# Columns by TensorE transpositions, Gram steps at other slots, idle products in the first inverse, and output copies in halves, in a delta-rule attention with an FFN

## The chip, the cores and the metric

The kernel runs on one core of one Trainium2 chip. The metric is the time of one execution on the device, in microseconds; three executions of the kernel before were timed, and one more was profiled. TensorE (PE) multiplies, VectorE (DVE) and ScalarE (ACT) do the elementwise work, GpSimd (POOL) next to nothing, and SyncE (SP) issues nearly all DMA transfers from one queue in order.

## The reference

Attention by the delta rule over 4 sequences of 768 tokens, 8 heads of 48 columns, and behind it a feed-forward layer (FFN) over all 3072 tokens, 384 to 2048 to 384:

```python
def _attn_ref(q, k, v, beta):
    k_n = k / (np.linalg.norm(k, axis=-1, keepdims=True) + 1e-06)
    state = np.zeros((B, H, D, D), dtype=np.float32)
    for t in range(S):
        kt, vt, bt = (k_n[:, :, t], v[:, :, t], beta[:, :, t, None])
        y[:, :, t] = np.einsum('bhd,bhde->bhe', q[:, :, t], state)
        v_old = np.einsum('bhde,bhd->bhe', state, kt)
        state = state + bt[:, :, :, None] * np.einsum('bhd,bhe->bhde', kt, vt - v_old)
    return y

def _moe_ref(x, w_in, w_out):        # x: the attention's y, heads side by side
    h = x @ w_in
    g = np.maximum(0.01 * h, h)
    return g @ w_out
```

## The kernel before

**Blocks.** The sequence is cut into 12 blocks of 64 tokens; a block takes these 64 tokens of all four sequences, so the FFN of a block n sees 256 tokens. For each block the steps are:

- *Gram* (`gram`, pg L284): products k k^T and k q^T of the block. ACT copies them (gs, L288), eight DMAs gd<-gs (L292) write the part for the inverse to DRAM, and two L<-gd (L307) read it back in the inverse's layout. For blocks 0 and 1 `first` does this.
- *Inverse* (`inv`): norms and scales (`norms`, L324 and on), a memset of the buffer T (L367; there is one T), then 31 elimination steps on VectorE (`eliminate`, L348 multiplies, L353 subtracts), each for the two 32 x 32 triangular halves of every head and sequence. At the end ACT copies T into the other layout (L402), and SP writes both to DRAM (td L409, tt L410). One inverse covers blocks 0 and 1 together, then there is one for each block.
- *Join* (`merge_z`, `merge_u`): SP reads tt and td back as block-diagonal tiles sq (four sq<-tt L466, four sq<-td L469) and into rt (L475); sixteen products pz and sixteen pu (`product`, L437) make the off-diagonal quarter of the inverse.
- *Solve* (`solve`): products pk, pw, pc, py (L561, L577, L587, L597) with copies on ACT between them (rt L563, rv L579 and L589), in two halves (g = 0 and 1) of the heads. The last gives y, which ACT copies into ys (L599), 128 tokens a half, 384 columns in fp32.
- *Columns* (`columns`): y has to stand with its columns on the partitions. Six fp32 products of 128 x 128, ys as the stationary operand and the unit matrix `eye` as the moving one, write px (L627; three column groups by two halves). ACT casts px to xh (L119), VectorE makes the rest xl = px - xh (L120), both fp32r.
- *FFN* (`ffn`): for each of 16 f, nine products ph of 256 columns (L656; xh and xl by the two parts of w_in), ACT makes gh (L661) and the leaky ReLU in place (L662), VectorE gl, the rest (L664); two f later six products po of 384 columns (L646), three for each half of the tokens, sum into po_0 and po_1. In the end ACT copies these into ob (L676), and four DMAs write the rows to the output (L679).

Weights come as 64-bit words and are cut into parts on VectorE and ACT (L144 to L177), some before the first FFN and the rest beside it.

**What sets the order.** `weave` calls the steps of several streams by slots: in the loop over n, 17 slots, one for each f and one for the end of the FFN. Beside the FFN of block n run the solve of block n + 1 (slots by SV), the inverse of block n + 2 (slots by IV, the entry n of it) and a Gram step for block n + 2 (slots by GG, for n = 0 to 2); from n = 2 on another Gram step, for block n + 3, runs at slot 12. `behind(name)` holds an instruction back until the last one so marked has been issued. From these calls a scheduler with a model of the engines makes the order in which every engine and queue runs; within an engine nothing overtakes.

The lines that set the slots are:

```python
IV, GG = ((7, 17), (8, 17), (8, 17), (2, 17)), ((0, 2), (3, 4), (1, 2))   # L731
SV = (0, 9), (3, 11), (2, 11)
```

Of the kernel before, what the change touches and what calls it, by code (L numbers as in the profile page):

```python
# [9 lines left out]
F32 = mybir.dt.float32  # L10
# [10 lines left out]
C = 64  # L21
# [9 lines left out]
HC = C // 2  # L31
P = 128
# [14 lines left out]
def delta_moe_kernel(ctx: ExitStack, tc, kq0, kqT, kv, qT, beta, cst, w_all, out, nblk):  # L47
# [10 lines left out]
    nc = tc.nc  # L58
    NFC, _, DO = w_all.shape[1:]
    NCC = DO // P  # L60
    NTB = TB // P
# [6 lines left out]
    ps_a = ctx.enter_context(tc.tile_pool(name="ps_a", bufs=4, space=PSUM))  # L68
# [6 lines left out]
    eye = csb[:, C:C + P]  # L75
# [5 lines left out]
    neg = st.tile([P, P], F32R, name="neg")  # L81
# [32 lines left out]
    def behind(name):  # L114

        return tc.issue_after(mark[name]) if name in mark else nullcontext()

    def split(src, hi, lo):
        mark["xh"] = nc.scalar.copy(hi, src).ins  # L119
        return nc.vector.tensor_tensor(lo, src, hi.bitcast(F32), ALU.subtract)  # L120
# [44 lines left out]
    def lows():  # L165
        while True:
            f, g, t = later.pop(0)
            if f in BYV:
                nc.vector.tensor_tensor(t[:, 2 * DO:], g, t[:, 0:2 * DO].bitcast(F32), ALU.subtract)
# [10 lines left out]
    Lh, gm, nrm, Tts, zs, ys, xs, done = {}, {}, {}, {}, {}, {}, {}, set()  # L180

    def need(gen, fn, n):
        while (fn, n) not in done:
            next(gen)
# [153 lines left out]
    def eliminate(b, L, j, T, m):  # L338


        w = HC - 1 - j
        parts = []
        for x in range(min(m, 2)):
            t = T[:, x:m:2]
            k = t.shape[1]
            tv = sb.tile([P, 144], F32, tag=f"tmp{x}", name=f"tmp{b}_{j}_{x}", bufs=1)
            tv = tv[:, 0:k * w].rearrange("p (x w) -> p x w", x=k)
            nc.vector.tensor_tensor(  # L348
                tv, t[:, :, j:j + 1].broadcast_to([P, k, w]),
                L[:, j, j + 1:].rearrange("p (o w) -> p o w", o=1).broadcast_to([P, k, w]), ALU.mult)  # L350
            parts.append((tv, t[:, :, j + 1:]))
        for tv, t in parts:
            mark["steps"] = nc.vector.tensor_tensor(t, t, tv, ALU.subtract).ins  # L353

    def inv(b):

        if b:
            need(gg, gram, NB[b][0])
        two = len(NB[b]) > 1
        M = HC if two else HC // 2  # L360
        X = sb.tile([P, HC * HC], F32, tag="T", name=f"T{b}", bufs=1)
        T = X[:, 0:M * HC].rearrange("p (m i) -> p m i", m=M)
        if two:
            nc.gpsimd.memset(T, 0.0)
        else:
            with behind("gl"):
                nc.vector.memset(T, 0.0)  # L367
        yield
        L = Lh.pop(b)
        c = norms(b, L.rearrange("p m i -> p (m i)")[:, ::HC + 1])  # L370
        if two:
            nc.vector.tensor_copy(X[:, ::HC + 1], c)
        else:
            for e in range(2):
                r = slice(e * 64, e * 64 + 64)
                nc.vector.tensor_copy(X[r, e:M * HC:HC + 2], c[r, e::2])
        for x in range(2):
            l = L[:, x * HC // 2:(x + 1) * HC // 2]
            nc.vector.tensor_tensor(l, l, c.rearrange("p (o i) -> p o i", o=1).broadcast_to(list(l.shape)), ALU.mult)
        if two:  # L380
            for n in NB[b]:
                lengths(n)
        yield
        for j in range(HC - 1):
            eliminate(b, L, j, T, j + 1 if two else j // 2 + 1)
            if j == HC - 2:
                if two:
                    Tc = sb.tile([P, HS, HC], F32, tag="L", name="tc", bufs=2)
                    nc.vector.transpose(Tc.rearrange("p l i -> p i l"), T.rearrange("p m i -> p i m"))
                    for i, n in enumerate(NB[b]):  # L390
                        Tts[n] = Tc, T[i * 64:i * 64 + HC]
                    for g in range(NGR):
                        place(0, g, 1)
                    d = nc.vector.transpose(T, T)
                    mark["inverse"] = d.ins
                    for g in range(NGR):
                        d = place(0, g, 0)
                    mark["inverse"] = d.ins
                else:
                    n = NB[b][0]  # L400
                    Tt = X[:, M * HC:].rearrange("p (i m) -> p i m", m=M)
                    nc.scalar.copy(Tt.rearrange("p i m -> p m i"), T)  # L402
                    td = dr.tile([2, HC, HS, HC], F32, tag="td", name=f"td{n}")
                    tt = dr.tile([HS, HC, HC], F32, tag="tt", name=f"tt{n}")
                    Tts[n] = td, tt
                    for x in range(2):
                        a = x * 64
                        for e in range(2):
                            nc.sync.dma_start(td[e, x::2].rearrange("m l i -> l m i"), T[a + e * HS:a + (e + 1) * HS])  # L409
                        nc.sync.dma_start(tt.rearrange("l i (x m) -> x l i m", m=M)[x], Tt[a:a + HS])  # L410
                done.add((inv, b))
            yield
# [119 lines left out]
    def solve(n):  # L532
        b = where[n][0]
        need(iv, inv, b)
        if n >= 2:
            lengths(n)
# [82 lines left out]
    def columns(n):  # L619

        need(sv, solve, n)
        xs[n] = parts = []
        px = [ps_a.tile([P, 2, TB], F32, tag="a", name=f"px{n}_{i}") for i in range(2)]
        part = [px[cc // 2][:, cc % 2] for cc in range(NCC)]
        for cc, x in enumerate(part):
            for g in range(NGR):
                i = nc.tensor.matmul(x[:, g * P:(g + 1) * P], ys[n, g][:, cc * P:(cc + 1) * P], eye, start=True, stop=True)  # L627
        mark["px"] = i.ins
        for cc, x in enumerate(part):
            xh, xl = (sb.tile([P, TB], F32R, tag=t, name=f"{t}{n}_{cc}", bufs=3) for t in ("xh", "xl"))  # L630
            i = split(x, xh, xl)
            if not n:
                mark["x"] = i.ins
            parts.append((xh, xl))

    def ffn(n):
        need(sv, solve, n)
        x = xs.pop(n)
        po = [ps_o.tile([P, 512], F32, tag=f"o{t}", name=f"po{n}_{t}") for t in range(NTB)]
        pend = []  # L640

        def second(f, gh, gl):
            for t in range(NTB):
                ts_ = slice(t * P, (t + 1) * P)
                for k, (a, w) in enumerate(((gh, wo[0]), (gh, wo[1]), (gl, wo[0]))):
                    i = nc.tensor.matmul(  # L646
                        po[t][:, :DO], a[:, ts_], w[f],
                        start=(f == 0 and k == 0), stop=(f == NFC - 1 and k == 2))
            mark["po"] = i.ins

        for f in range(NFC):
            ph = hbank[f % 2][:, f // 2 % 2]
            k = 0
            for cc in range(NCC):
                for a, e in ((wi[0], 0), (wi[0], 1), (wi[1], 0)):
                    i = nc.tensor.matmul(ph, a[f][:, cc * P:(cc + 1) * P], x[cc][e], start=(k == 0), stop=(k == 3 * NCC - 1))  # L656
                    k += 1
            mark["ph"] = i.ins
            gh = sb.tile([P, TB], F32R, tag="gh", name=f"gh{n}_{f}", bufs=FB)
            gl = sb.tile([P, TB], F32R, tag="gl", name=f"gl{n}_{f}", bufs=FB)  # L660
            nc.scalar.activation(gh, ph, AF.Prelu, alpha=0.01)  # L661
            i = nc.scalar.activation(ph, ph, AF.Prelu, alpha=0.01)  # L662
            mark["h"] = i.ins
            i = nc.vector.tensor_tensor(gl, ph, gh.bitcast(F32), ALU.subtract)  # L664
            mark["gl"] = mark[f"gl{f}"] = i.ins
            pend.append((f, gh, gl))
            if len(pend) > PD:
                second(*pend.pop(0))
            yield
        if n + 1 < nblk:  # L670
            columns(n + 1)
        for a in pend:
            second(*a)
        for t in range(NTB):
            ob = sb.tile([P, DO], F32, tag="ys", name=f"ob{n}_{t}", bufs=3)
            nc.scalar.copy(ob, po[t][:, :DO])  # L676
            for a in range(0, P, C):
                r0 = (t * P + a) // C * nblk * C + n * C
                nc.sync.dma_start(out[r0:r0 + C], ob[a:a + C])  # L679
        yield  # L680

# [45 lines left out]

WAHEAD, WEARLY = 4, 8
BYV = (0, 1) + tuple(range(3, 16, 2))
KA, KB, WB = 4, 2, 12  # L730
IV, GG = ((7, 17), (8, 17), (8, 17), (2, 17)), ((0, 2), (3, 4), (1, 2))  # L731
LL, AG = 2, 6
SV = (0, 9), (3, 11), (2, 11)
PD, FB = 2, 3
# [65 lines left out]
```

## Time and profile before

| | us |
|---|---|
| median of three runs (lowest, highest) | 657.07 (655.5, 658.13) |
| the profiled execution | 655.7 |
| its span from the first to the last instruction | 653.6 |
| TensorE busy | 602.4 (92%) |
| VectorE busy | 443.1 (68%) |
| ScalarE busy | 332.4 (51%) |

The mean granted clock of TensorE is 0.993 of full. The page cuts the span into 40 slices of 16.3 us; a digit is the busy share in tenths:

```
PE   5258999989979989999999999999999999999996
DVE  3999999987645969749749749659559559222221
```

TensorE is idle in part of the first 50 us, where the weights are cut, the first inverse runs and the first solve waits for it. From the fourth slice on it is near full, with thinner slices between 100 and 240 us, and it is full from 250 us to the end. VectorE is full in the first 145 us and then again in every inverse.

### The profile page before, as it was taken

To read this page: it belongs to the slowest core of one execution; us is meant where nothing else is said; L and a number is where in the kernel's file an instruction comes from. 1 tells how busy PE (TensorE), PEld (TensorE's weight loads), DVE (VectorE), ACT (ScalarE), POOL (GpSimd) and SP (SyncE) were. 2 spreads that over 40 slices of the span, in tenths; PEclk is the share of its full clock that TensorE was granted. 3 is DMA by queue.
4 is the path that set the end of the run, shared out by engine and by line. 5 is a ranking of instruction groups with operands and counts; after the bars stand their busy time and mean duration, and the time that the engine had idled before them with its cause. 6 is when DMAs were issued, how large, how long until landed. Compare 5 with 4: busy or idle time off the path is not lost.

```text
span 653.6 us, 19762 instructions
## 1 busy us (share of the span) xinstructions
PE 602.4 (92%) x7762; PEld 563.1 (86%) x7762; DVE 443.1 (68%) x1994; ACT 332.4 (51%) x855; POOL 10.7 (2%) x17
## 2 busy tenths in 40 slices
PE   5258999989979989999999999999999999999996
PEld 4156789988869979999999999999999999999996
DVE  3999999987645969749749749659559559222221
ACT  3456999334526445545545545445445445444322
POOL 6000000000000000000000000000000000000000
PEclk9998999999999999999999999999999999999999
DMA  5983953152453551461571660660660640400101
GB/s 122 292 252 115 242 203 75 26 121 35 100 99 56 132 96 30 87 128 41 107 122 28 118 134 3 119 134 4 126 127 7 123 78 15 75 19 2 26 0 25
DMA packets 124572, 59.51 MB, mean 91 GB/s; under 512 B 111424, under 2 KB 114624, under 8 KB 124480
## 3 DMA queue, kind: packets, MB, share of 16 engines
q1 hardware_dynamic: 124064, 57.73, 40.7%
q8 instruction: 61, 1.00, 0.7%
q10 hardware_dynamic: 416, 0.53, 0.4%
q14 instruction: 31, 0.25, 0.1%
HBM read 46.96 MB, written 11.27 MB: 89 GB/s over the span
## 4 chain that ended last, share of the span: by engine, by line
PE 85%; DMA 6%; DVE 3%; ACT 2%; issue 2%; SPq 1%; ACTq 0%
PE ph L656 32%; PE po L646 30%; PE pw L577 3%; PE pk L561 3%; PE py L597 3%; PE pg L284 3%; PE pc L587 3%; PE px L627 2%; DMA rv<-in_kv 2%; DMA kq<-in_kqT 2%; PE wl L175 1%; DMA wr<-in_w_all 1%; PE pz L437 1%; DVE rq L299 1%; PE pu L437 1%
## 5 line engine op out<-in xcount | busy, mean ns | idle before, releaser
L656 PE MATMUL ph<-xh,w 128*128 128x256 f32 x1152 | 246.3, 290 | 3.5 <-DVE gl L664 3.0
L656 PEld LDWEIGHTS ph<-xh,w 128*128 128x128 f32 x1152 | 191.0, 189 | 13.6 <-DVE gl L664 4.6
L646 PE MATMUL po<-w,gh 128*128 128x384 f32 x768 | 188.6, 343 | 4.1 <-ACT gh L661 4.1
L664 DVE TENSOR_TENSOR gl<-ph,gh 128x256 fp32r<-128x256 f32 x192 | 80.5, 422 | 160.5 <-ACT ph L662 157.4
L656 PE MATMUL ph<-xl,w 128*128 128x256 f32 x576 | 162.1, 283 | 0.8 <-DVE xl L120 0.8
L661 ACT ACTIVATE gh<-ph 128x256 fp32r<-128x256 f32 x192 | 73.7, 384 | 172.8 <-PE ph L656 170.7
L646 PEld LDWEIGHTS po<-w,gh 128*128 128x128 f32 x768 | 132.5, 188 | 7.6 <-ACT gh L661 6.2
L646 PE MATMUL po<-w,gl 128*128 128x384 f32 x384 | 115.6, 338 | 0.0
L353 DVE TENSOR_TENSOR T<-T,tmp 128x60 f32<-128x60 f32 (+35 forms) x661 | 112.4, 207 | 0.8
L348 DVE TENSOR_TENSOR tmp<-T,L 128x60 f32<-128x60 f32 (+35 forms) x661 | 112.2, 208 | 0.7
L656 PEld LDWEIGHTS ph<-xl,w 128*128 128x128 f32 x576 | 109.0, 189 | 1.9 <-DVE xl L120 1.4
L662 ACT ACTIVATE ph<-ph 128x256 f32<-128x256 f32 x192 | 73.1, 381 | 0.0
L646 PEld LDWEIGHTS po<-w,gl 128*128 128x128 f32 x384 | 66.7, 189 | 0.2 <-issue 0.2
L299 DVE TENSOR_TENSOR rq<-pg,csb 64x256 f32<-64x256 f32 x80 | 33.8, 423 | 9.3 <-ACT gs L288 8.0
L579 ACT COPY rv<-pw 64x384 f32<-64x384 f32 x48 | 22.7, 473 | 18.2 <-PE pw L577 17.3
L563 ACT ACTIVATE rt<-pk 48x512 f32<-48x512 f32 x44 | 26.1, 592 | 10.2 <-PE pk L561 9.4
L597 PE MATMUL py<-rv,rq 128*64 128x48 f32 x768 | 28.0, 225 | 0.7 <-issue 0.7
L577 PEld LDWEIGHTS pw<-rv,rt 128*64 128x64 f32 x768 | 25.3, 145 | 3.0 <-ACT ph L662 2.1
L589 ACT COPY rv<-pc 48x384 f32<-48x384 f32 x44 | 20.8, 474 | 13.6 <-PE pc L587 13.3
L577 PE MATMUL pw<-rv,rt 128*64 128x48 f32 x768 | 27.1, 230 | 0.0
L597 PEld LDWEIGHTS py<-rv,rq 128*64 128x64 f32 x768 | 25.7, 140 | 1.1 <-issue 0.9
L627 PE MATMUL px<-csb,ys 128*128 128x128 f32 x144 | 22.1, 288 | 2.0 <-ACT ys L599 2.0
(90 smaller groups left out, 553.0 us busy)
## 6 DMA issues: line engine op xcount, KB each, us to landing
wr<-in_w_all SPq DMA_DIRECT2D x16, 768.0 KB, 7.4
kq<-in_kqT SPq DMA_DIRECT2D x40, 192.0 KB, 5.4
L<-gd SPq DMA_DIRECT2D x20, 256.0 KB, 3.9
rk<-in_kv SPq DMA_DIRECT2D x24, 192.0 KB, 4.0
rv<-in_kv SPq DMA_DIRECT2D x24, 192.0 KB, 4.2
rq<-in_qT SPq DMA_DIRECT2D x24, 192.0 KB, 4.3
out<-ob SPq DMA_DIRECT2D x48, 96.0 KB, 3.2
gd<-gs SPq DMA_DIRECT2D x80, 32.0 KB, 1.7
```

Of the source, the lines that this page charges most:

```text
L299: nc.vector.tensor_tensor(qa[DN, c, b * NPAIR:(b + 1) * NPAIR], pv[b][r, 1], tri[r].rearrange("p (o t) -> p o t", o=1).broadcast_to([C, NP ...
L348: nc.vector.tensor_tensor(tv, t[:, :, j:j + 1].broadcast_to([P, k, w]), L[:, j, j + 1:].rearrange("p (o w) -> p o w", o=1).broadcast_to([P ...
L353: mark["steps"] = nc.vector.tensor_tensor(t, t, tv, ALU.subtract).ins
L563: nc.scalar.mul(t[UP, c], pv[c * 64:c * 64 + D].rearrange("p (y v) t -> p y v t", y=2), -1.0)
L577: nc.tensor.matmul(pv[r, u], t[:, c, u // NPAIR, u % NPAIR], v[:, c, u], start=True, stop=True)
L597: nc.tensor.matmul(pv[s * C:(s + 1) * C, u * D:(u + 1) * D], qa[:, c, u], v[:, c, u], start=True, stop=True)
L627: i = nc.tensor.matmul(x[:, g * P:(g + 1) * P], ys[n, g][:, cc * P:(cc + 1) * P], eye, start=True, stop=True)
L646: i = nc.tensor.matmul(po[t][:, :DO], a[:, ts_], w[f], start=(f == 0 and k == 0), stop=(f == NFC - 1 and k == 2))
L656: i = nc.tensor.matmul(ph, a[f][:, cc * P:(cc + 1) * P], x[cc][e], start=(k == 0), stop=(k == 3 * NCC - 1))
L661: nc.scalar.activation(gh, ph, AF.Prelu, alpha=0.01)
L662: i = nc.scalar.activation(ph, ph, AF.Prelu, alpha=0.01)
L664: i = nc.vector.tensor_tensor(gl, ph, gh.bitcast(F32), ALU.subtract)
```

## The change

Four edits:

1. The columns px come from `nc.tensor.transpose` with the same operands in place of a product with `eye`. There are 72 of them.
2. The slots of block 3's Gram step move from (3, 4) to (1, 2) of n = 1 and block 3's inverse starts at slot 6 rather than 8; block 4's Gram step moves from (1, 2) to (3, 4) of n = 2.
3. In the last block the remaining po are called by token halves, the copy of each half into ob is cut in two (ACT and VectorE, 64 tokens each), and the output DMAs go from SP and from ACT.
4. `warm` issues one small product that reads T (or its transposed copy) and 8, 7 and 3 products neg x neg of 512 columns whose result nobody reads, behind the elimination steps 20 and 30 and the transposition of T in the first inverse.

```diff
+    def warm(x, count):
+        ps = ps_a.tile([P, 512], F32, tag="a", name="warm")
+        nc.tensor.matmul(ps[:, 0:HC], eye, x, start=True, stop=True)
+        for i in range(count):
+            nc.tensor.matmul(ps.rearrange("p (o t) -> p o t", t=P), neg,
+                             neg.rearrange("p (o t) -> p o t", o=1).broadcast_to([P, 4, P]), start=True, stop=True)
...
         for j in range(HC - 1):
             eliminate(b, L, j, T, j + 1 if two else j // 2 + 1)
+            if two and j in WARM:
+                warm(T[:, 0], WARM[j])
...
                     nc.vector.transpose(Tc.rearrange("p l i -> p i l"), T.rearrange("p m i -> p i m"))
+                    warm(Tc[:, 0], WARM[HC])
...
-                i = nc.tensor.matmul(x[:, g * P:(g + 1) * P], ys[n, g][:, cc * P:(cc + 1) * P], eye, start=True, stop=True)
+                i = nc.tensor.transpose(x[:, g * P:(g + 1) * P], ys[n, g][:, cc * P:(cc + 1) * P], eye)
...
-        def second(f, gh, gl):
-            for t in range(NTB):
+        def second(f, gh, gl, tiles=range(NTB)):
+            for t in tiles:
...
-        for a in pend:
-            second(*a)
+        last = n + 1 == nblk
+        if not last:
+            for a in pend:
+                second(*a)
         for t in range(NTB):
+            if last:
+                for a in pend:
+                    second(*a, tiles=(t,))
             ob = sb.tile([P, DO], F32, tag="ys", name=f"ob{n}_{t}", bufs=3)
-            nc.scalar.copy(ob, po[t][:, :DO])
-            for a in range(0, P, C):
+            for i, a in enumerate(range(0, P, C)):
                 r0 = (t * P + a) // C * nblk * C + n * C
+                if last:
+                    (nc.vector.tensor_copy if i else nc.scalar.copy)(ob[a:a + C], po[t][a:a + C, :DO])
+                    (nc.scalar if i else nc.sync).dma_start(out[r0:r0 + C], ob[a:a + C])
+                    continue
+                if not i:
+                    nc.scalar.copy(ob, po[t][:, :DO])
                 nc.sync.dma_start(out[r0:r0 + C], ob[a:a + C])
...
+WARM = {HC - 12: 8, HC - 2: 7, HC: 3}
-IV, GG = ((7, 17), (8, 17), (8, 17), (2, 17)), ((0, 2), (3, 4), (1, 2))
+IV, GG = ((7, 17), (6, 17), (8, 17), (2, 17)), ((0, 2), (1, 2), (3, 4))
```

What this makes of the engines' order is seen at three places. In these lists a line number is that of its own kernel (the lines of the changed one stand 8 to 11 further, L402 there is L413), and numbers behind names are those of buffers.

SP's queue at the join of block 3, before: td and tt are written, read back as sq and rt, with block 4's eight gd<-gs in two rows of four among them.

```order
L410 DMA tt_2823<-T_2322 1024x1x16
L475 DMA rt_82<-td_2822 32x16x32
L475 DMA rt_83<-td_2822 32x16x32
L469 DMA sq_2156<-td_2822 32x8x32
L466 DMA sq_2154<-tt_2823 32x8x32 x3
L292 DMA gd_2867<-gs_0_2868 32x8x32 x4
L292 DMA gd_2867<-gs_1_2900 32x8x32 x4
L466 DMA sq_2154<-tt_2823 32x8x32
L469 DMA sq_2156<-td_2822 32x8x32
L307 DMA L_2866<-gd_2867 64x1024 x2
```

SP's queue at the same place in the changed kernel:

```order
L421 DMA tt_2847<-T_2264 1024x1x16
L518 DMA rk_77<-in_kv 64x768
L480 DMA sq_2180<-td_2846 32x8x32
L700 DMA out<-ob_0_2819 64x384 x2
L700 DMA out<-ob_1_2823 64x384 x2
L477 DMA sq_2178<-tt_2847 32x8x32 x4
L480 DMA sq_2180<-td_2846 32x8x32 x3
L486 DMA rt_82<-td_2846 32x16x32 x2
L486 DMA rt_83<-td_2846 32x16x32 x2
L518 DMA rv_84<-in_kv 64x768
```

The four sq<-tt stand together, and the eight gd<-gs (six rows on) behind the whole join; four output DMAs and one load of rk now stand ahead of the sq<-tt.

ACT at the end of the FFN of n = 1, before: the copies of block 2's solve, the copy of T at the end of block 3's inverse (L402), the output copies of n = 1 and the casts of block 2's columns.

```order
L589 COPY rv_86<-pc_0_2449 48x384 x2
L599 COPY ys_0_2485<-py_0_2468 128x384
L589 COPY rv_87<-pc_1_2487 48x384 x2
L599 COPY ys_1_2523<-py_1_2506 128x384
L402 COPY T_2322<-T_2322 128x16x32
L676 COPY ob_0_2789<-po_0_1987 128x384
L676 COPY ob_1_2793<-po_1_1988 128x384
L119 CAST xh_0_2765<-px_0_2757 128x256
```

The same place in the changed kernel:

```order
L600 COPY rv_86<-pc_0_2503 48x384 x2
L413 COPY T_2264<-T_2264 128x16x32
L610 COPY ys_0_2539<-py_0_2522 128x384
L600 COPY rv_87<-pc_1_2541 48x384 x2
L610 COPY ys_1_2577<-py_1_2560 128x384
L699 COPY ob_0_2819<-po_0_2011 128x384
L699 COPY ob_1_2823<-po_1_2012 128x384
L119 CAST xh_0_2795<-px_0_2787 128x256
```

The copy of T, which waits for the last elimination step of block 3's inverse, has moved ahead of both ys. At the end of n = 2 the same copy for block 4's inverse moves from behind the three casts and both ob copies to ahead of them.

TensorE at the end of the program, before: the last po behind the last ph.

```order
L646 MATMUL po_0_10056<-w_1508,gl_14_10336 128x384
L646 MATMUL po_1_10057<-w_1508,gl_14_10336 128x384
L646 MATMUL po_0_10056<-w_1516,gh_15_10355 128x384 x2
L646 MATMUL po_1_10057<-w_1516,gh_15_10355 128x384 x2
L646 MATMUL po_0_10056<-w_1516,gl_15_10356 128x384
L646 MATMUL po_1_10057<-w_1516,gl_15_10356 128x384
```

The same place in the changed kernel:

```order
L657 MATMUL po_0_10080<-w_1532,gl_14_10360 128x384
L657 MATMUL po_1_10081<-w_1532,gl_14_10360 128x384
L657 MATMUL po_0_10080<-w_1540,gh_15_10379 128x384 x2
L657 MATMUL po_1_10081<-w_1540,gh_15_10379 128x384 x2
L657 MATMUL po_0_10080<-w_1540,gl_15_10380 128x384
L657 MATMUL po_1_10081<-w_1540,gl_15_10380 128x384
```

Nothing has moved: the two halves still take turns.

## Rows read from the trace of the kernel before

**Rows 1.** Stretches: start:end, length, busy by engine (instructions), PEclk, DMA share, GB/s.

```profile
100.00:150.00 50.00, 47.44 (x426) 45.01 (x422) 44.77 (x191) 25.68 (x64) 0.00 (x0) 1.00 0.36 77
300.00:400.00 100.00, 99.12 (x1293) 93.32 (x1292) 71.69 (x365) 50.45 (x133) 0.00 (x0) 1.00 0.43 84
```

**Rows 2.** Waits of TensorE: line, what it waited for: total us, times, longest.

```profile
PE pz L454 <- ACT rt L420: 20.1, 1, 20.1
...
PE pz L437 <- DMA sq<-tt: 1.4, 1, 1.4
```

**Rows 3.** Chain that ended last, block 3's join: start, us, what.

```profile
189.16 3.77 issue
...
193.80 2.22 PE ph L656 x9
196.02 1.21 PE po L646 x5
```

**Rows 4.** Chain that ended last: first columns, plain groups of ph and po, later columns.

```profile
53.29 2.93 PE px L627 x12
...
187.04 1.07 PE ph L656 x9
188.11 1.05 PE po L646 x6
...
329.23 0.67 PE px L627 x6
```

**Rows 5.** Timeline of SP's queue: start, us, line, operation, out<-in, count.

```profile
186.51 3.90 SPq L292 DMA_DIRECT2D gd<-gs  x8
...
244.53 2.02 SPq L466 DMA_DIRECT2D sq<-tt  x4
```

**Rows 6.** Stretches at the lower clock (the eighth number is the clock).

```profile
54.00:55.00 1.00, 1.00 (x7) 1.00 (x6) 1.00 (x2) 0.00 (x0) 0.00 (x0) 0.50 0.02 8
...
194.50:196.00 1.50, 1.50 (x9) 1.50 (x8) 0.00 (x0) 0.00 (x0) 0.00 (x0) 0.50 1.09 202
```

**Rows 7.** Instructions of tile px: ns least/median/most, first to last start.

```profile
L627 PEld LDWEIGHTS px<-csb,ys x144: 187/192/333, 53.3 to 609.6; 128*128 128x128 f32 x144
L627 PE MATMUL px<-csb,ys x144: 270/275/580, 53.3 to 609.7; 128*128 128x128 f32 x144
```

**Rows 8.** Timeline of ACT and VectorE at the first columns; brackets: idle before.

```profile
51.03 1.70 ACT L156 CAST w<-cg 128x768 fp32r<-128x768 f32 x2 [2.08 <-DVE cg L152]
52.76 0.86 ACT L599 COPY ys<-py 128x384 f32<-128x384 f32 x2
...
55.45 0.95 DVE L152 SCALAR_TENSOR_TENSOR cg<-wr,cg 128x768 uint32<-128x768 uint32 x1
56.44 0.42 DVE L120 TENSOR_TENSOR xl<-px,xh 128x256 fp32r<-128x256 f32 x1
57.30 0.76 DVE L120 TENSOR_TENSOR xl<-px,xh 128x256 fp32r<-128x256 f32 x2 [0.44 <-ACT xh L119]
```

**Rows 9.** Timeline of VectorE, ACT and TensorE: inverses 2 and 3, block 2's join.

```profile
141.96 0.16 DVE L353 TENSOR_TENSOR T<-T,tmp 128x8 f32<-128x8 f32 x1
148.06 0.48 DVE L367 MEMSET T<- 128x512 f32 x1 [0.70 <-DMA tt<-T]
...
173.80 1.09 ACT L402 COPY T<-T 128x512 f32<-128x512 f32 x1 [1.06 <-DVE T L353]
...
151.76 0.65 PE L437 MATMUL pz<-sq,gm 128*32 128x128 f32 x16 [1.36 <-DMA sq<-tt]
176.79 0.50 PE L656 MATMUL ph<-xh,w 128*128 128x256 f32 x2 [0.45 <-ACT xh L119]
```

**Rows 10.** Timeline of VectorE: the first and the last row of inverse 4.

```profile
207.13 0.48 DVE L367 MEMSET T<- 128x512 f32 x1
...
236.01 0.17 DVE L353 TENSOR_TENSOR T<-T,tmp 128x8 f32<-128x8 f32 x1
```

**Rows 11.** Timeline of SP's queue: the last output DMAs.

```profile
648.47 2.39 SPq L679 DMA_DIRECT2D out<-ob  x4
```

## Prediction

> **What bounds the kernel now.** I read the table of stretches first, for which engine is full where. Between 300 and 400 us TensorE is busy 99.12 of 100 us; between 100 and 150 it is 47.44 of 50 with VectorE at 44.77 of 50 [rows 1]. So after block 4 only less work on TensorE shortens the run, and before it the small waits count. The waits of TensorE [rows 2] say which: 20.1 us in the first inverse (nothing to multiply yet), 1.4 for block 2's join (pz behind sq<-tt). The dearest is not under its true name: the chain shows 3.77 us of "issue" from 189.16, then the sixteen pz of block 3's join, then nine ph in 2.22 us [rows 3] where nine take 1.07 and six po 1.05 [rows 4]. That "issue" is a transfer: in SP's queue eight gd<-gs of block 4's Gram step hold 186.51 to 190.41, ahead of the fourth sq<-tt [rows 5]. Behind the wait TensorE's granted clock was 0.50 of full, its lower level of 1.2 GHz, in 194.50 to 196.00 [rows 6]; the nine ph lost 1.15, and the five po behind them, 1.21 for 0.88 [rows 3, 4], another 0.33: 1.5 in all.
>
> **The change, part by part.** All sums are against the profiled run's own 655.7 us (span 653.6 and 2.1 around it); the median is 657.07, 1.4 above, which is added at the end.
>
> *Columns.* A logical px product is two records, 144 records for 72 products. Six records took 0.67 us in the chain [rows 4]: 0.22 a product, 1.31 a block. The records themselves last 275 ns, with loads of 192 [rows 7], but they overlap. Each product becomes one transposition, with the same operands; before has none. Bounds of its pace: a ph product of 256 columns takes 1.07/9 = 0.119, so 128 columns take 0.06 at best; two px records, 0.22, if nothing changes; and 0.467 (192 + 275) if neither load nor stream overlaps. I take 0.075, near the ph end, since a px record, half a product, is paced at 0.11 and one of the two goes. Saved: 1.31 − 0.45 = 0.86 a block, between +0.95 and −1.5. At the late blocks it lies wholly on the path: n = 4 to 11, 8 × 0.86 = 6.9. The Trainium skill, "TensorE: Matmul & The Clock Gate", section "Terms", calls its transpose mode four times faster for FP32: 0.22/4 would be 0.055, and eight blocks would give 7.8. The Trainium skill's same page, "Part 4: PE-mode transpose", speaks against the change: about 275 ns for a 128 × 128 transposition inside a kernel, 48 × 0.275 = 13.2 us against 10.5 now, a loss; no row here shows a transposition on TensorE.
>
> *The head.* The first columns took 2.93 us at the half clock [rows 4, 6], and here some 2 go. But ACT's ys copy (52.76) stands behind two weight casts that wait for VectorE, and the first xl (56.44) stands behind VectorE's L152 of 0.95 [rows 8]; its row shows no idle time ahead of it. All three xl then run together, ending about 57.6 for 58.06: 0.4 gained.
>
> *Idle products.* Eighteen of 512 columns, each about two ph (0.24 us; 0.48 at the half clock): 4.3 to 9 us, inside the 20.1 idle. The next elimination step that writes T must wait for the small product that reads it; other VectorE rows stand between. Whatever they speed up or hold up ends at the same two queues of the head: 0, with bounds of ±0.5, one such step or two.
>
> *Block 2's join and block 3's Gram steps.* Gram of block 3 goes from slots 3–4 of n = 1 to 1–2, and its norms ahead of the memset. Inverse 2 ends at 142.12, the join's pz ran at 151.76, 9.6 later [rows 9]. pz now stand one f later, with 9 ph and 10 po more ahead (1.07 + 1.75 = 2.8): the 1.36 wait disappears, and that with px and the head puts TensorE 2.7 ahead there. Little of it lasts, for inverse 3 then ends late. Before: memset 148.06; ACT's copy, which waits for the last step, starts at 173.80 [rows 9]. Its norms are done early, so its steps begin some 2.6 sooner: end at about 171.1 rather than 173.77. On ACT the copy of T (1.09) and both ob copies stood behind the second ys; now the copy of T stands ahead of the first ys. So from 171.1: copy 1.09, ys 0.48, rv 0.95, py and ys of the second half about 1.0, ob 0.96, the first xh 0.38: 176.0, and ph starts there rather than at 176.79 [rows 9]. Gain at this boundary: **0.8**, between 0 and 3.
>
> *Block 4's Gram steps behind block 3's join.* In SP's order the eight gd<-gs leave the join; its four sq<-tt stand together. The wait of 3.77 goes and with it the clock's 1.5; pz also stand one f earlier, so I leave 0.4 of waiting. Gain 5.27 − 0.4 = 4.9, now **5.7** ahead, and with px of n = 3 **6.6**.
>
> *What is late next: inverse 4.* It ran from 207.13 to 236.18, 29.05 us [rows 10]. Starting 5.7 sooner, with about 1.5 less of gl and xl among its steps, it ends near 229.0. Before, its ACT copy stood behind the xh of n = 3; now ahead of them, so ph of n = 3 can't start before 229.0 + 1.09 + 0.38 = 230.5. In the trace of before, TensorE had by 235.6 done as much as it must have done by then; 6.6 ahead, that is 229.0. Wait: **1.5**. Then the join: block 4's pz stand behind f 4 rather than f 6. Their transfers want 12.4 us from the inverse's end (236.18 to 248.6: the sq<-tt were issued until 246.55 [rows 5], landing some 2 later); TensorE gets there in 1.5 (copy and xh) + five ph groups (5.35) + 18 po (3.15) + 0.9 for the start and the norms' product = 10.9. Wait: **1.5**. Left of the 6.6: 3.6.
>
> *The tail.* TensorE's order of the last f is word for word as before, po_0 and po_1 in turn: that part of the change doesn't do what it says, and is worth 0. What it does: half of the ob copies go to VectorE and two of four output DMAs to ACT's queue. SP's four took 2.39 after the copies [rows 11], 0.6 each; two go, less the second ACT copy ahead of ACT's: 0.75, between 0 and 1.2.
>
> Sum: 3.6 (head to n = 3) + 6.9 (n = 4 to 11) + 0.75 = 11.25. 655.7 − 11.25 + 1.4 = **645.8**.
>
> **The rivals.**
> 1. *VectorE doesn't bind.* If inverses 3 and 4 end early enough: 0.4 (head) + 9.5 (px, 11 × 0.86) + 1.4 and 4.9 (the two joins) + 0.75 = 17.0, 640.1. For: once inverse 5 runs, TensorE is 99% busy beside the same work of VectorE. Against: 44.77 of 50 [rows 1], and the ACT copies of T that now stand ahead of ys and of xh.
> 2. *A transposition is as dear as the product it replaces* (0.22). The columns give nothing: 11.25 − 6.9 = 4.35, less some 0.45 where n = 2 and 3 were held by TensorE: 3.9, 653.2. For: the load of 128 fp32 columns stays. Against: half the records go.
> 3. *0.275 each, the record's own length* [rows 7]: 3.9 − 48 × 0.055 = 1.3: 655.8, within 0.5%. Against: px records are paced at 0.11. (The Trainium skill's Part 4, above, states the same price.)
> 4. *Block 4's join falls as late as block 3's did*, with the clock falling behind it: 1.5 again and 2 more of waiting, 649.3. For: it moves two f's forward. Against: SP's queue is clear of gd<-gs there.
> 5. *Slower: a transposition overlaps neither with its load nor with its neighbour.* 0.467 each, 48 × 0.249 = 12.0 lost instead of 6.9 gained: 655.7 − 3.9 + 12.0 + 1.4 = 665.2. It decides from 0.22 + 3.9/48 = 0.30 each. Against: 144 records overlap today.
>
> **How the numbers follow.** Forecast 645.8 (its own range 642 to 649.5): 0.50. Rival 1 0.16, rival 2 0.11, rival 3 0.05, rival 4 0.13, rival 5 0.05. The range reaches rival 1 on one side, with the lower bound of the pace (8 × 0.09 = 0.7), and rivals 4 and 2 on the other: 638.5 to 653. A measurement here tells about 0.5% from no change, 653.8 to 660.4. Faster holds the forecast, rivals 1 and 4 and nearly all of rival 2: 0.88; same, rival 3 and the rest of 2: 0.07; slower 0.05.
>
> **What would show it.** px in groups of six at 0.35 to 0.65 us in the chain between 300 and 400 us (right), at 1.3 or more (rivals 2, 3, 5). No "issue" in front of the pz of block 3, and no half clock around 195. ph of n = 2 waiting for xh at about 176, ph of n = 3 for xh near 230 behind ACT's copy of T, and pz of block 4 waiting for sq<-tt by 1 to 2 us (none: rival 1; over 3 with a half clock: rival 4). The last SP row of out<-ob with two transfers in about 1.2 us. The forecast is wrong if TensorE's busy time outside px changes, or if n = 4 to 11 shorten by less than 5 us.

## The result, and the profile after

The changed kernel takes 646.32 us (median of four runs, 645.93 to 646.67) beside 656.55 of the kernel before (four runs): 0.9842 of its time, 95% interval 0.982 to 0.9864. The forecast was 645.8 with a range of 638.5 to 653. The profiled execution took 646.5 us, its span 644.7; before it was 655.7 and 653.6.

The page after, busy us by engine and the busy tenths of TensorE, VectorE and the granted clock in 40 slices (16.1 us each):

```profile
PE 602.8 (93%) x7714; PEld 561.5 (87%) x7714; DVE 443.5 (69%) x1996; ACT 331.7 (51%) x855; POOL 10.7 (2%) x17
...
PE   4287999989999889999999999999999999999996
...
DVE  3999999988645968749749749659659659222221
...
PEclk9998999989989989999999999999999999999999
```

TensorE's busy time is as before (602.4, now 602.8): the columns px went from 22.1 to 12.3 us of it, and the idle products brought 9.6. Outside the two it is 0.7 more, and the clock row has three slices of 8 between 129 and 242 us, where before has 9 throughout.

Waits of TensorE after (line, what it waited for: total us, times, longest), against [rows 2]:

```profile
PE ph L667 <- DVE gl L675: 6.1, 2, 3.7
...
PE po L657 <- ACT gh L672: 2.9, 10, 0.3
PE px L638 <- ACT ys L610: 2.2, 2, 1.2
...
PE ph L667 <- DVE xl L120: 1.9, 1, 1.9
PE ph L667 <- ACT xh L119: 1.0, 2, 0.7
```

Neither join appears: the 1.4 of block 2 and the 3.77 us of "issue" ahead of block 3's pz [rows 2, 3] are gone. Behind gl stand 6.1 us, where it was 3.0 before (twice, the longest 2.3): the new wait is the one of 3.7.

The tile px after, against [rows 7], and the chain of a late block, against [rows 4]:

```profile
L638 PEld LDWEIGHTS px<-csb,ys x72: 137/141/226, 54.2 to 600.5; 128*128 128x128 f32 x72
L638 PE MATMUL px<-csb,ys x72: 270/273/418, 54.2 to 600.6; 128*128 128x128 f32 x72
```

```profile
325.58 0.66 PE px L638 x6
326.24 2.10 PE po L657 x12
```

Six transpositions, a whole block, take 0.66 us. Before, six records took 0.67, but they were three products. So a transposition is one record, it lasts as long as one did (273 ns) and is paced at 0.11.

Over the late blocks this can be measured without choosing a row: sixty-four pw of the solve open every block, here blocks 5 and 11 (before, then after):

```profile
307.81 2.07 PE L577 MATMUL pw<-rv,rt 128*64 128x48 f32 x64
592.89 2.07 PE L577 MATMUL pw<-rv,rt 128*64 128x48 f32 x64
```

```profile
304.61 2.07 PE L588 MATMUL pw<-rv,rt 128*64 128x48 f32 x64
585.10 2.07 PE L588 MATMUL pw<-rv,rt 128*64 128x48 f32 x64
```

285.08 us became 280.49: 4.59 over six blocks, 0.77 a block, so 6.1 for eight. The first pw is 3.20 earlier, of which one block's 0.77 (n = 4) belongs to the late part: the stretch up to the end of n = 3 gave some 2.4, although the first product came 0.60 us later in this profile (4.94 for 4.34). From the end of the last po to the end of the span it was 5.44 us (648.11 to 653.55) and is 5.05 (639.66 to 644.71): 0.39.

### The profile page after: what moved, and what is told of

It reads as the page before. It is cut to its first block, busy times and chain, and to the rows that moved or that the text cites. A ratio compares the mean times of both kernels' runs of the same rounds, so it can differ in the third digit from the quotient of the medians.

```text
span 644.7 us, 19679 instructions
## 1 busy us (share of the span) xinstructions
PE 602.8 (93%) x7714; PEld 561.5 (87%) x7714; DVE 443.5 (69%) x1996; ACT 331.7 (51%) x855; POOL 10.7 (2%) x17
## 4 chain that ended last, share of the span: by engine, by line
PE 78%; DVE 11%; DMA 5%; SPq 2%; issue 2%; ACT 1%; DVEq 0%; ACTq 0%
PE ph L667 30%; PE po L657 29%; PE pw L588 3%; PE pk L572 3%; PE py L608 3%; DVE tmp L348 3%; DVE T L353 2%; PE pc L598 2%; PE pg L284 2%; PE px L638 1%; DMA wr<-in_w_all 1%; PE wl L175 1%; DMA kq<-in_kqT 1%; PE pz L448 1%; PE pu L448 1%
## 5 line engine op out<-in xcount | busy, mean ns | idle before, releaser
L667 PEld LDWEIGHTS ph<-xl,w 128*128 128x128 f32 x576 | 110.3, 192 | 2.3 <-DVE xl L120 2.1
L120 DVE TENSOR_TENSOR xl<-px,xh 128x256 fp32r<-128x256 f32 x36 | 14.3, 421 | 18.2 <-ACT xh L119 18.2
```

## The experiments

All twelve runs. "Before" is the kernel before, timed beside them.

| run | what it is | us | before | ratio, 95% interval |
|---|---|---|---|---|
| px_only | before + edit 1 | 651.5 | 655.9 | 0.9928 (0.9894 to 0.9961) |
| no_px | changed - edit 1 | 655.05 | 655.9 | 0.9982 (0.9961 to 1.0003) |
| no_warm | changed - edit 4 | 648.28 | 655.9 | 0.9872 (0.9839 to 0.9905) |
| no_slots | changed - edit 2 | 647.66 | 655.9 | 0.9857 (0.9828 to 0.9886) |
| slots_only | before + edit 2 | 653.49 | 656.0 | 0.9956 (0.9941 to 0.9972) |
| g5_late | changed, block 5's Gram step later | 643.87 | 656.0 | 0.9822 (0.9805 to 0.9839) |
| px_twice | changed, transpositions doubled | 652.31 | 656.0 | one run |
| halves | changed, po by token halves on TensorE | 644.13 | 656.0 | one run |
| best | g5_late and halves | 643.11 | 656.25 | 0.9805 (0.9788 to 0.9823) |
| best_nowarm | best - edit 4 | 645.28 | 656.25 | 0.9838 (0.9821 to 0.9855) |
| best_t | best, copy of T behind ys | 646.41 | 656.25 | 0.9858 (0.9845 to 0.9872) |
| warm_only | before + edit 4 | 655.64 | 656.25 | 0.9995 (0.998 to 1.0011) |

**Edit 1 alone, and edit 1 undone.**

```diff
-i = nc.tensor.matmul(x[:, g * P:(g + 1) * P], ys[n, g][:, cc * P:(cc + 1) * P], eye, start=True, stop=True)
+i = nc.tensor.transpose(x[:, g * P:(g + 1) * P], ys[n, g][:, cc * P:(cc + 1) * P], eye)
```

> The kernel before with edit 1 alone (columns by transpositions). Theory: the changed kernel's trace shows six transpositions in 0.66 us against 1.31 for six products, 0.65 a block; the eight late blocks lie wholly on the path, 8 x 0.65 = 5.2 us, and of the four early ones little: 650 to 651.5 beside 656.5, the chain from 250 us on shorter by 5.2, the 3.8 us stall ahead of block 3's pz still there. Rival 1 (the slots made the gain, the columns are hidden): within 2 us of 656.5. Rival 2 (as forecast, 0.075 a transposition): 8 x 0.86 = 6.9, below 649.6.

> The changed kernel with edit 1 undone (columns by products with eye again). Theory: 5.2 us from the eight late blocks come back, and up to 2.6 from the early four: 651.5 to 654 beside 646.3; six px records pairs at 1.3 us a block. Rival 1 (the slots made the gain): within 2 us of 646.3. Rival 2 (0.075 each was on the path, with a loss elsewhere): 653 or more with the early part unchanged.

Alone it gave 4.4 us, a bit less than the 5.2 named; undone it cost 8.7, more than the 7.8 named. Both rivals that put the gain elsewhere fall: the columns are most of it. The time of no_px is also what its rival 2 named (653 or more), but not for its reason: a block of the late part gains 0.77 and not 0.86. That part repeats: from pw of block 5 to pw of block 11 no_px needs 285.06 us, as before (285.08), and px_only 280.27 (280.49 in the changed kernel). The difference between 4.4 and 8.7 is made ahead of block 4. There the scheduler orders other rows differently too when px changes (on VectorE and ACT from 60 us on), so what a transposition is worth in the early blocks is not shown, and the runs scatter (648.94 to 654.85, and 652.47 to 657.9).

**The transpositions doubled.** The same instruction twice, into the same place, in the changed kernel.

```diff
-                i = nc.tensor.transpose(x[:, g * P:(g + 1) * P], ys[n, g][:, cc * P:(cc + 1) * P], eye)
+                for _ in range(2):
+                    i = nc.tensor.transpose(x[:, g * P:(g + 1) * P], ys[n, g][:, cc * P:(cc + 1) * P], eye)
```

> The changed kernel with each transposition issued twice into the same place: 72 more on TensorE. Theory (0.11 us each on the path): the eight late blocks take 48 x 0.11 = 5.2 us more than in the changed kernel between the first pw of n = 4 and the end, and the 1.3 us a block of the products before the change are reached. Rival 1 (as forecast, 0.075): 3.6 more. Rival 2 (the load sets the pace, and a second one with the same operand is cheaper, or latency does): under 2, or over 10.

```profile
305.00 2.07 PE L588 MATMUL pw<-rv,rt 128*64 128x48 f32 x64
589.77 2.07 PE L588 MATMUL pw<-rv,rt 128*64 128x48 f32 x64
```

These are the same two pw: 284.77 us, 4.28 more than in the changed kernel for 36 transpositions, 0.119 each. That is the theory's 0.11 and not the forecast's 0.075, and two of them cost what a product cost.

**Edit 2 undone, and edit 2 alone.**

```diff
-IV, GG = ((7, 17), (6, 17), (8, 17), (2, 17)), ((0, 2), (1, 2), (3, 4))
+IV, GG = ((7, 17), (8, 17), (8, 17), (2, 17)), ((0, 2), (3, 4), (1, 2))
```

> The changed kernel with edit 2 undone (slots of the Gram steps and of inverse 3 as before). Theory: the slots brought 4.7 us at block 3's pz and lost about 1.5 of them again to a half-clock stretch behind 136 and to TensorE waiting for gl at 223: without them 649 to 651, the stall of 3 to 4 us ahead of block 3's pz back. Rival (what the slots win at the join is lost again by the half-clock stretches, net nothing): 646 to 647.5.

> The kernel before with edit 2 alone (slots of the Gram steps and of inverse 3). Theory after the run with the slots undone: the stall of 3.8 us ahead of block 3's pz goes, and what it gives is lost again to TensorE waiting for gl near 225 and at the columns of n = 2; net 0 to 1.5 us, 654.5 to 656.5. Rival (as the prediction had it, 4.9 us at the join and about half of it kept): 653.5 or less.

The theory of the first of these fell: without the slots the kernel is 1.3 us slower, not 3 to 5, and since the two intervals overlap not even the 1.3 is sure. TensorE's rows at block 3's pz without them, and its waits:

```profile
193.95 0.64 PE L448 MATMUL pz<-sq,gm 128*32 128x128 f32 x16 [4.03 <-DMA sq<-tt]
```

```profile
PE ph L667 <- DVE gl L675: 3.7, 2, 2.5
```

The stall at the join is back in full, but the wait for gl shrinks from 6.1 to 3.7. Edit 2 alone took 2.5 us off the kernel before, above the 0 to 1.5 that I then expected: it is the rival's 653.5, half of the prediction's 4.9. There TensorE waits 6.8 us for gl. Of what edit 2 saves at the join, a good part is waited for again forty us later. The next run shows on what.

**Block 5's Gram step later.** In the changed kernel TensorE stands at 223.40 for 3.74 us. VectorE's rows at that time (start, us, operation, out<-in), then TensorE's:

```profile
219.88 0.86 DVE L299 TENSOR_TENSOR rq<-pg,csb 64x256 f32<-64x256 f32 x2
...
221.03 0.86 DVE L299 TENSOR_TENSOR rq<-pg,csb 64x256 f32<-64x256 f32 x2
221.90 0.58 DVE L304 COPY gm<-gs 32x256 f32<-32x256 f32 x2
...
223.27 0.86 DVE L299 TENSOR_TENSOR rq<-pg,csb 64x256 f32<-64x256 f32 x2
...
224.54 0.86 DVE L299 TENSOR_TENSOR rq<-pg,csb 64x256 f32<-64x256 f32 x2
225.42 0.58 DVE L304 COPY gm<-gs 32x256 f32<-32x256 f32 x2
...
226.66 0.42 DVE L675 TENSOR_TENSOR gl<-ph,gh 128x256 fp32r<-128x256 f32 x1
...
227.14 0.39 PE L667 MATMUL ph<-xh,w 128*128 128x256 f32 x1 [3.74 <-DVE gl L675]
```

The gl of f 13 could have run at about 220.6, when ACT had left its ph (gh at 219.91, the in-place pass at 220.19 for 0.38). In VectorE's order it stands behind the eight rq and four gm of block 5's Gram step, with steps of inverse 4 between them: 6 us. The ph of f 15 needs the PSUM bank that this gl reads. So block 5's step was moved in the loop over n:

```diff
-              (gg, NGR * (1 < n < nblk - 3), 12, 13))
+              (gg, NGR * (1 < n < nblk - 3), *((15, 17) if n == 2 else (12, 13))))
```

> The changed kernel with block 5's Gram step at slots 15 to 16 of n = 2 rather than 12; in VectorE's order its eight rq and two gm then stand behind the last gl of n = 2 rather than ahead of gl of f 13. In the changed kernel TensorE waited 3.74 us at 223.40 for that gl (3.27 with the columns alone, 1.25 with the old slots), and a half-clock stretch followed at 228.5. Theory (VectorE's order, not the join, sets the stretch from 200 to 240): the wait falls under 1.5 and 1.5 to 4 us are won, 642.5 to 645. Rival (TensorE then waits as long for the xl of n = 3, which stand behind the same rq, or for the join of block 4): 645.5 to 647.5.

643.87, 2.4 less than the changed kernel, though the two were timed apart and their intervals overlap (0.9805 to 0.9839, and 0.982 to 0.9864). Its waits of TensorE:

```profile
PE ph L667 <- DVE gl L675: 3.3, 3, 2.4
PE px L638 <- ACT ys L610: 2.2, 2, 1.3
```

The long wait for gl is gone; the 2.4 us left are those at 132. Of the rival's waits, xl after the head and the join, none appears. So VectorE's order between 200 and 230 us was what edit 2's gain ran into: taking it away removes the wait, and best below shows the gain once more.

**Token halves in TensorE's order.** As the prediction says, the order did not follow the code. Holding the second half back does it:

```diff
                 for a in pend:
-                    second(*a, tiles=(t,))
+                    with behind("po") if t else nullcontext():
+                        second(*a, tiles=(t,))
```

> The changed kernel with the last po of the second token half held behind those of the first in TensorE's order (twelve po, now six and six). Theory: po_0 is done 1.05 us sooner, its copy and one transfer on each queue start sooner, and the last two transfers are issued 0.6 us after the last copy rather than 1.2: 0.5 us off the time behind the last ph, if nothing else holds them. Rival (ACT's queue has both copies ahead of its first transfer, so it stays where it is): 0 to 0.1 us.

From the end of the last po (638.05) to the end of the span (642.34) it took 4.29 us, for 5.05 in the changed kernel: 0.76. More than the theory's 0.5; the rival falls, although ACT's two transfers do start behind both copies. SP issues its first transfer already at 637.54, ahead of the last po's end:

```profile
637.54 1.51 SPq L697 DMA_DIRECT2D out<-ob  x2
```

This run has a second use. Up to the last twelve po its instructions stand in exactly the changed kernel's order, so up to there the two profiles are one program run twice. From 132 to 177 us TensorE waits for the same rows equally long, and still this run is 2.1 us ahead at 177. TensorE's rows of the changed kernel, then of this one, with the stretches (the eighth number is the granted clock):

```profile
135.20 0.39 PE L667 MATMUL ph<-xh,w 128*128 128x256 f32 x1 [2.35 <-DVE gl L675]
...
177.13 0.66 PE L667 MATMUL ph<-xh,w 128*128 128x256 f32 x2 [0.68 <-ACT xh L119]
...
137.00:139.00 2.00, 2.00 (x8) 1.80 (x8) 2.00 (x17) 0.44 (x2) 0.00 (x0) 0.50 0.12 23
```

```profile
134.53 0.39 PE L667 MATMUL ph<-xh,w 128*128 128x256 f32 x1 [2.35 <-DVE gl L675]
...
175.02 0.51 PE L667 MATMUL ph<-xh,w 128*128 128x256 f32 x2 [0.68 <-ACT xh L119]
...
137.00:139.00 2.00, 2.00 (x16) 2.00 (x16) 2.00 (x16) 0.55 (x2) 0.00 (x0) 1.00 0.03 8
```

After the same idle 2.35 us the granted clock fell to its lower level (1.2 GHz) in one run and not in the other. 0.67 us apart before, 2.11 apart after: one such stretch cost 1.44 us. Not all of it lasts: this run, ahead at 177, then waits 4.48 us for the gl of f 13, where the changed kernel waits 3.74.

**The two together, and two things more.** best is g5_late with halves. best_nowarm leaves the idle products out of it. best_t holds ACT's copy of T, which edit 2 brought ahead of ys, behind ys again:

```diff
-                    nc.scalar.copy(Tt.rearrange("p i m -> p m i"), T)
+                    with behind("ys"):
+                        nc.scalar.copy(Tt.rearrange("p i m -> p m i"), T)
```

> The changed kernel with block 5's Gram step at slots 15 to 16 of n = 2 and the last po by token halves in TensorE's order, both together. Theory: the two are at different places and add up: 2.5 (646.3 to 643.9) + 0.8 (the time from the last po to the end fell from 5.0 to 4.25 us): 642 to 644, and half-clock stretches ahead of block 4 (none to four in a run) spread the runs by 1 to 1.5 us each. Rival (the gain of the late Gram step was a run with few half-clock stretches): 645 to 646.5.

> As the run best, with edit 4 undone (no idle products). Theory: the idle products bring nothing that lasts, since the first columns wait for VectorE and ACT in any case: within 1 us of best. Rival (the run without them was 2 us slower than the changed kernel because they keep the clock up where the first FFN begins): 1.5 to 2.5 us more than best, with more half-clock stretches or a slower first FFN until the first ph of n = 1.

> As the run best, with ACT's copy of T (end of each inverse) held behind the ys copies of the solve beside it, as it stood in the kernel before. Theory (the copy of T ahead of ys costs the columns of n = 2 a wait, 0.92 us for px and 0.68 for ph in the changed kernel's trace): both waits under 0.5 us, 0.5 to 1.5 us off best. Rival (block 3's join, whose td and tt then start later, waits instead): pz of block 3 waits 1 us or more, no gain.

best takes 643.11 us (641.51 to 644.01), 0.9805 of before: the theory held, and this version beats both kernels (its slowest run is under the changed kernel's fastest, 645.93, though that was timed on another occasion). best and halves differ in the late Gram step alone: the last po ends at 635.44 us in best's profile and at 638.05 in that of halves, 2.6 apart, of which the one half-clock stretch of halves behind 62 us (at 225, behind its wait for gl) is a part. best_t fails as its rival said, 3.3 us worse. The wait ahead of px falls from 0.92 to 0.25, but that of ph rises from 0.68 to 1.26, and the join waits again:

```profile
190.41 1.08 PE L449 MATMUL pz<-sq,gm 128*32 128x128 f32 x16 [2.97 <-DMA sq<-tt]
```

So ahead of ys the copy of T costs the columns next to nothing (1.60 us of waits, and 1.51 behind ys) and saves the join 3: its new place is right. The profile of best_t also has a half-clock stretch at 135.6 that best's has not, which is the rest or part of it.

**The idle products.** Edit 4 taken out of the changed kernel (no_warm) and of best, and put alone into the kernel before.

```diff
-            if two and j in WARM:
-                warm(T[:, 0], WARM[j])
...
-                    warm(Tc[:, 0], WARM[HC])
```

> The changed kernel with edit 4 undone (no idle products). In the changed kernel's trace the last ten idle products ran at 0.47 us each from 38.6 to 43.6 and the first pz, free at about 41.3, stood behind them until 43.58 (40.34 before). Theory: they cost the head up to 2.3 us at the first pz, of which 0 to 1.5 last, and bring nothing: 645 to 646.3. Rival (they hold the clock up for the first solve and pay for themselves): 647 or more, with pw of block 0 slower than now (now 3.2 us from the first pw to the first py).

> The kernel before with edit 4 alone (the idle products). Theory: nothing that lasts, 655 to 657; the first pz some 2 us later, the first columns as late as before. Rival (they hold the clock up for the first solve and FFN): 654 or less.

Alone they do nothing that can be measured (0.9995, interval across 1); the first pz comes at 40.97 us there, 0.63 later than before and not the 2 named. Taken out they cost 2.0 us in the changed kernel and 2.2 in best, against the theory. The first is not sure: the intervals overlap, and no_warm's runs fall into two pairs (646.76 and 647.17, 649.38 and 649.6). best_nowarm was timed beside best (643.58 to 645.82 against 641.51 to 644.01). The size is the rivals', the reason (the clock at the first solve and the first FFN) is not: from the first pw to the first py no_warm takes 3.0 us for 3.2, and block 1's pw come earlier without the products (90.88 us in best_nowarm, 91.67 in best). The changed kernel's rows show no gain where they stand:

```profile
38.61 3.33 PE L360 MATMUL warm<-neg 128*128 128x512 f32 x7
41.74 0.47 PE L358 MATMUL warm<-tc,csb 128*128 128x32 f32 x2
42.02 1.63 PE L360 MATMUL warm<-neg 128*128 128x512 f32 x3
43.58 1.44 PE L465 MATMUL pz<-rt,gm 32*32 32x32 f32 x64
```

The first pz ran at 40.34 before; now it stands behind the idle products until 43.58. The first ph came at 55.61, and at 55.37 without them. Where the two traces part is later: without them block 3's pz waits for sq<-tt, 1.41 us in no_warm and 1.06 in best_nowarm, where with them it does not wait; and the profile of best_nowarm has a half-clock stretch at 135.6 us that best's has not. But the scheduler, given or not given these products, also orders the weights' casts of n = 0 (ACT's rows from 60 to 110 us) and VectorE's rows up to 170 us differently, in no_warm those of n = 2 too. Whether the products, that order or the clock of single runs are worth the 2 us was not told apart.

## Why the prediction was right, point by point

The time came out 0.5 us above the forecast and inside the range. The steps behind it were not all right, and that it came so near is in part luck. The three terms, forecast at 3.6 + 6.9 + 0.75 = 11.25, were some 2.4 + 6.1 + 0.4 = 8.9 between the two profiled runs. What closed the gap is the 1.4 that I added because the median before lay that far above the profiled run: in the changed kernel median and profiled run are the same (646.32 and 646.5), and against the latter the sum alone, 644.45, was 2 us too low.

**Columns: mechanism right, size off.** I took 0.075 us a transposition; 0.11 in the chain and 0.119 when doubled are the measured ones. The term that was mis-sized is "near the ph end": the nearest row was the other one, a px record at 0.11, and a transposition is paced just like it. The late blocks gave 6.1 us, not 6.9. The six instructions explain 0.65 of the 0.77 a block; the other 0.12 stays open. On the Trainium skill, "TensorE: Matmul & The Clock Gate": the "four times faster for FP32" of its "Terms" is two times here (1.31 to 0.66 a block). The 275 ns of its "Part 4: PE-mode transpose" (given there beside a figure for bf16) are the length of a record here too (273, in fp32), but in a row they overlap, so it was no price.

**Head: nothing gained; idle products: right as a sum.** The first ph came 0.64 us sooner, but the forecast's 0.4 was for the three xl, and the next ph waits for them. The rows of TensorE and VectorE after, where before the last two xl ran from 57.30 to 58.06 [rows 8]:

```profile
57.97 0.58 PE L667 MATMUL ph<-xl,w 128*128 128x256 f32 x1 [1.86 <-DVE xl L120]
```

```profile
58.36 0.76 DVE L120 TENSOR_TENSOR xl<-px,xh 128x256 fp32r<-128x256 f32 x2 [0.44 <-ACT xh L119]
```

They ended at 59.12, not at 57.6, 1.06 later than before; 0.60 of that is the later first product, and with the idle products alone (warm_only) they end at 58.72. Behind the wait the clock fell, and at the columns of n = 1 TensorE was 0.48 us later than before (114.01 for 113.53). The idle products alone are 0, as forecast. That they delay the first pz (43.58 for 40.34 here, 40.97 in warm_only) I did not see: I looked at what they hold up on VectorE, not at what stands behind them on TensorE.

**Block 2's join: wait gone, lead missing.** I forecast TensorE 2.7 us ahead there. pz ran at 154.28 with 2.8 us more done, for 151.76: 0.3 ahead. The wait for gl at 132 (2.35, for 2.26 before) stayed, and in this run the clock fell behind it, 1.44 us.

**Columns of n = 2: right in kind.** ph was to wait for xh at 176.0. It waited (0.92 for ys and 0.68 for xh) and started at 177.13, and at 175.02 in the second run of the same order. Of the 2.11 between the two, 1.44 is the half-clock stretch and 0.67 an earlier start.

**Block 3's join: right.** No "issue", no wait; in SP's rows the four sq<-tt run together (181.50 to 183.57), with nothing of block 4's Gram step among them.

**Inverse 4: the step that failed.** I named ACT: its copy of T ahead of xh, then the join, 1.5 us each. Neither was waited for. Inverse 4 ended at 231.36 rather than 229.0, the copy ran at 231.40 and xh at 232.29, but TensorE had po until 233.5. I had looked up where the copy of T moved, and not where gl stands on VectorE. That wait, 3.74 us, is by luck of the size of my two together (3.0): that the forecast's 3.6 for the head to n = 3 comes within 1.2 of the 2.4 measured is compensation. The rest is not accounted for row by row; the half-clock stretches (behind 56 us four, at 57.9, 136, 177 and 229, for one at 193 before) and the later first product are in it.

**The tail: right in kind, too large.** 0.39 for 0.75; that the token halves had no effect was right too, and halves shows what they are worth, 0.76.

**The rivals.** Rival 1 (VectorE doesn't bind, 640.1) is wrong for the changed kernel; best goes half of the way, 643.1. Rival 2's pace of 0.22 is refuted by the rows, as are 3 and 5; rival 4's late join did not come. The prediction's sign of being wrong, TensorE's busy time outside px, moved by the 9.6 of the idle products, which it counts by themselves (4.3 to 9), and by 0.7 more.

## What to carry to other kernels

When a change clears a stall, look in each engine's new order for the row that the next consumer needs, here gl behind eight rq, and not only for the instructions that the change names. A stall that is gone is worth only part of its length until the engine that runs full in the same stretch gives its rows in the order in which they are waited for. To price an instruction that the trace doesn't show, take the nearest record's pace, and measure it by issuing it twice. Where a scheduler orders the program anew, an edit taken out alone is not one change: compare the orders before the times.

## What was not expected of the hardware

- The same order of instructions, with the same waits up to 177 us, ran once with four half-clock stretches behind 56 us and once with two (the changed kernel and halves). Each fall of the changed kernel came in or behind a wait of TensorE (1.86, 2.35, 0.92 and 0.68 together, and 3.74 us), but not each such wait brought one: in best the waits of 2.34 and of 0.92 and 0.68 brought none. A stretch where TensorE was wanted cost 1.44 us, so single profiles of a kernel with early waits differ by more than some of its edits.
- The idle products of 512 columns ran at 0.47 us each (3.33 for seven), twice the 0.24 that two ph of 256 columns take, while the profile gives a granted clock of 1.00 for that time:

```profile
33.00:36.00 3.00, 3.00 (x8) 2.04 (x7) 3.00 (x21) 3.00 (x15) 0.00 (x0) 1.00 1.02 409
```

  The pace says the lower level there, and the kernel before settles it: within the sixty-four py of block 0 the pace doubles, from 0.069 to 0.035 us each, while the granted clock reads 1.00 for both stretches.

```profile
47.66 1.51 PE L597 MATMUL py<-rv,rq 128*64 128x48 f32 x22
49.85 1.48 PE L597 MATMUL py<-rv,rq 128*64 128x48 f32 x42 [0.69 <-issue]
```

  The first clock record in that trace, a rise to full, stands at 49.86 us; in the changed kernel's it stands at 44.20, behind the last idle product. Ahead of its first record the trace holds nothing on the clock, and the 1.00 shown there is no reading.
